# A gated-layer kernel: inner products in two more places, and the weight sums they need made one chunk earlier

## The chip, the core and the metric

The kernel runs on one core of one Trainium2 chip. The metric is device time in microseconds of one execution, lower is better. The engines of the core are written as in the profile: PE (matrix products), PEld (its weight loads), DVE (element-wise work on tensors), ACT (activations and copies), POOL (a second element-wise engine), SP (issues most DMAs). A tile has 128 partitions; "128x512" means 128 partitions by 512 elements.

## The reference

Four layers in a row on 2048 tokens of width 1024, each with a layer norm ahead of it and a residual behind it: linear attention, gated layer, linear attention, gated layer. Both attention layers share their weights, and both gated layers share theirs.

```python
def _B_ref(x, W_gate, W_up, W_down):          # the gated layer, F = 3584
    gate = einsum("bsd,df->bsf", x, W_gate)
    up = einsum("bsd,df->bsf", x, W_up)
    gate = gate * (gate > 0)
    return einsum("bsf,fd->bsd", gate * up, W_down)

x = x + _A_ref(_layernorm(x), A_wqkv, A_wo)   # layer 0 in the kernel
x = x + _B_ref(_layernorm(x), ...)            # layer 1
x = x + _A_ref(_layernorm(x), A_wqkv, A_wo)   # layer 2
x = x + _B_ref(_layernorm(x), ...)            # layer 3
```

## The kernel before

**Stages.** `run` calls `layer_A(0)`, `layer_B(1)`, `layer_A(2)`, `layer_B(3)`. A gated layer works on two chunks of 1024 tokens. This text writes (1,0) for the first chunk of layer 1, (1,1) for its second, and (3,0), (3,1) for those of layer 3. In each chunk there are 14 units `u` of 256 hidden columns (`glu`), and then the product with `W_down` (`down`), which adds its results onto the residual `x`.

**A unit.** Gate and up (`g` and `u` in names) are 2x2 block products in Winograd's form: seven block products instead of eight, numbered 1 to 7, each with one of seven combinations of weight blocks and of activation blocks (`s1` to `s4` are sums of activations). One block product is a group of four matmuls of 128x512 (`mm`, L1264). A unit is therefore 14 groups, in the order 5g 1g 5u 1u 2g 6g 2u 6u 7g 3g 7u 3u 4g 4u. The results pass through PSUM banks X, Y and Z: ACT copies X to Y (L1306), DVE makes Z from Y and product 5 (`zg`, `zu`, L1320), DVE adds product 5 to Y after product 7 (`m5g`, `m5u`, or `c22g`, `c22u` where product 5 comes from SBUF, L1340), and DVE's `put` (L1291) writes `h`. Because product 7 goes onto the same Y that Z is made from, group 7g must not start before `zg` is made, nor 7u before `zu`; and 4g and 4u must not start before `m5g` and `m5u` have read Y.

**Inner products.** In some units product 5 or 6 is not made by its own groups. For a pair of units (u, u+1) it is a 2x2 block product in itself, and is made by Winograd's form once more: seven inner products (`inner_gi`, L1117), each a group of four matmuls of 128x256, spread over the unit before the pair. They take the place of four groups of 128x512. The table `INNER` says where: product 5 in (3,0) for units 4 to 13 and in (3,1) for units 2 to 13; product 6 in (3,1) for units 3 to 12. Where product 6 comes from SBUF, DVE makes Y as X plus it (L1304) in place of ACT's copy.

Inner products need weight sums of a pair. `make_gi` makes them: eight DVE subtractions of 128x256 (L1072), DMAs of parts that exist already (`gi<-w`, L1075 and L1078), and one store of the subtractions' results (L1080). They are kept in DRAM as `gi5_u` and `gi6_u`, and `load_gi` (L1101) brings 896 KB of them back for each pair. Before the change the `gi5` are made in (1,1), with the still unused half of an `h` tile as the place of their results (named `h` in the profile), and the `gi6` in (3,0). `ready_gi` sets up a user of inner products: where the loaded sums lie, where results go (`V`), and four DVE sums of activations. For the places it uses tiles of `x` that have been sent away to DRAM (`send_away`, L274) and are brought back later (`bring_back`, L277).

**Weights.** In (1,0), `make_gu` makes a unit's four sums of weight blocks (L1172 to L1175, DVE) a unit ahead, and stores them as `tg`, `tu`. Later chunks load raw blocks (L1161) and sums (L1165); the sum that only product 5 or 6 uses is not loaded where that product is an inner one. Weights stand in a ring, five entries ahead.

**Order.** Code is written in the order of PE's work. `later.at(n, ...)` puts an action n ticks ahead, and a tick is one group of `mm`. `behind(last_put, ...)` asks that an action be scheduled after the last `put` made so far. A scheduler then fixes each engine's order when the program is built. DVE's order is thus a list that is known ahead of time, and so is SP's list of DMAs.

**Norms.** The layer norm ahead of layer 2 needs mean and variance of each 128-token tile `x[t]`: two `BATCH_NORM_STATS2` of 128x512 (L166) and one aggregate (L198). Before the change this was asked for from `down` of (1,1); the instructions for the first eight tiles stand among units 7 to 9 of (1,1), 564 to 591 us.

Of the kernel before, what the change touches and what calls it, by code (L numbers as in the profile page):

```python
# [14 lines left out]
P = 128  # L15
NW = 512
# [54 lines left out]
class _Later:  # L71
# [5 lines left out]
    def at(self, delay, fn):  # L77
        self.n += 1
        self.tasks.append((self.now + delay, self.n, fn))
# [13 lines left out]
class _Net:  # L93
# [93 lines left out]
    def ln_norm(self, layer, t):  # L187

        nc = self.nc
        if layer % 2:  # L190
            return self.ln_norm_sums(layer, t)
        src = self.xb[t] if layer == 0 else self.x[t]
        stats = self.small.tile([P, 2, nc.vector.BN_STATS_DIM], F32, tag="stats")
        for c in range(2):
            self.ln_stat(t, src, c, stats)
        if layer == 2:
            mv = self.small.tile([P, nc.vector.BN_AGGR_DIM], F32, tag="mv")
            nc.vector.bn_aggr(out=mv, in_=stats)  # L198
        else:
            mv, rstd = self.ln_rstd(stats)  # L200

        def scale(rstd=None if layer == 2 else rstd):
            if rstd is None:
                with self.tc.issue_after(self.last_exp.ins):
                    rstd = self.ln_root(mv)
                return lambda: scale(rstd)
            if layer % 2 == 0 and (layer, t // QT) != (2, 0):
                return self.ln_scale(src, mv, rstd, self.xn_home(layer, t))
            xn = self.temp([P, self.D], F16, name="xnb") if layer % 2 else self.xn_home(layer, t)
            shift = self.small.tile([P, 1], F32, tag="shift")  # L210
# [6 lines left out]
        return scale  # L217

    def ln_norm_sums(self, layer, t):

# [827 lines left out]
        for n in range(4):  # L1048
            self.later.at(at + 18 + 4 * n, lambda n=n: self.behind(self.last_put, lambda n: self.sums_dd(p, n), (n,)))

    INNER = {(3, 0): {5: range(4, 14)}, (3, 1): {5: range(2, 14), 6: range(3, 13)}}
    T_GU = {5: 0, 6: 2}

    def is_inner(self, l, c, u):
# [5 lines left out]
    def make_gi(self, l, c, m, u, at, out):  # L1060

        O = out.rearrange("p (n w k f) -> p n w k f", n=4, w=2, f=P)
        gi = self.gi[m, u]

        def block(w, a):
            return self.sums_gu(self.ring.get((l, c, w, u + a)))[:, self.T_GU[m]]

        def sums(n, w):
            b1, b2 = (block(w, a) for a in range(2))
            (b11, b21), (b12, b22) = ([b[:, 2 * j:2 * j + 2, :] for j in range(2)] for b in (b1, b2))  # L1070
            for o, a, b in ((0, b12, b11), (2, b22, b12), (1, b22, O[:, 0, n]), (3, b21, O[:, 1, n])):
                self.nc.vector.tensor_tensor(out=O[:, o, n], in0=a, in1=b, op=ALU.subtract)  # L1072

        for n, w in enumerate("gu"):
            self.later.at(at + n, lambda n=n, w=w: self.nc.sync.dma_start(  # L1075
                out=gi[:, 4:6, n, :, :], in_=block(w, 0).rearrange("p (j k) f -> p j k f", j=2)))
            self.later.at(at + 2 + 2 * n, lambda n=n, w=w: self.behind(self.last_put, lambda n: sums(n, w), (n,)))
            self.later.at(at + 4 + n, lambda n=n, w=w: self.nc.sync.dma_start(  # L1078
                out=gi[:, 6, n, :, :], in_=block(w, 1)[:, 2:4, :]))
        self.later.at(at + 6, lambda: self.nc.sync.dma_start(out=gi[:, 0:4, :, :, :], in_=O))  # L1080

# [496 lines left out]
    def plan_inner(self, l, c, u, hT):  # L1578

        at = self.later.at  # L1580
        ready = lambda m, *homes: self.behind(self.last_put, lambda m: self.ready_gi(l, c, m, *homes), (m,))
        if (l, c) == (1, 1):
            if u % 2 == 0 and u > 1:
                self.make_gi(l, c, 5, u, 2, hT[u // 2][:, 4:8, :].rearrange("p a n -> p (a n)"))
        if (l, c) == (3, 0):
            if u == 0:
                for n in range(4):
                    at(1 + 2 * n, lambda t=self.NS + n: self.send_away(t))
            if u == 2:
                self.inner_s = self.slot("gs", [P, 8 * NW], F16)  # L1590
                at(6, lambda: ready(5, 10, 8, self.inner_s[:, 0:4 * NW]))
            if u % 2 and 2 < u < self.U - 1:
                self.make_gi(l, c, 6, u, 2, self.inner_s[:, 4 * NW:8 * NW])
# [12 lines left out]
    def layer_B(self, l, final):  # L1606
        ring = self.ring
# [5 lines left out]
        for c in range(2):  # L1613
            hT = []
            first = l == 1 and c == 0
            wd = {}
            for u in range(self.U):
                if u % 2 == 0:
                    hT.append(self.slot(f"h{l}_{c}_{u // 2}", dtype=F16))
                ring.load_to(ring.index((l, c, "g", u)) + 5)  # L1620
                if first:
                    if u + 1 < self.U:
                        for n, w in enumerate("gu"):
                            self.later.at((4 if u else 9) + 4 * n, lambda u=u, w=w: behind(
                                self.last_put if u else self.last_z,
                                lambda: self.make_gu(ring.get((l, c, w, u + 1)), w, u + 1)))
                    if u == 3:
                        for d in (self.U - 4, self.U - 2):
                            wd[d] = self.load_d(d)
                        self.make_dd("22", 18)  # L1630
                    if u in (4, 5, 6):
                        for i, n in enumerate(range(3 * (u - 4), min(3 * (u - 3), 8))):
                            self.later.at(2 + 4 * i, lambda d=self.U - 4 + n // 4 * 2, n=n % 4: behind(
                                self.last_put, lambda: self.sums_d(wd[d], d, (n,))))
                    if u == 7:
                        self.make_dd("T1", 1)
                if not final and c == 1:
                    if u in (0, 3):
                        self.load_w("qk"[u // 3])
                    if u in (1, 2, 4, 5):  # L1640
                        for n in range(2):
                            self.later.at(4 + 5 * n, lambda w="qk"[u // 4], n=2 * (u % 3 - 1) + n: behind(
                                self.last_put, lambda: self.sums_w(w, n)))
                self.plan_inner(l, c, u, hT)
                if (l, c, u) in ((1, 1, 6), (3, 0, 5)):
                    self.make_dd("T4" if l == 1 else "21", 1)
                if c == 0 and u == 1:
                    for n, turn in enumerate(self.turns):
                        self.later.at(1 + n, turn)
                if c == 0 and u in (1, 2):  # L1650
                    self.later.at(6, lambda u=u: behind(self.last_put, self.pairs[u - 1]))
                self.glu(l, c, u, hT)
                if c == 0 and u == 2:
                    self.pairs[2]()
                if c == 0 and u == (self.U - 1 if first else 0):
                    after = self.last_put.ins
                if c == 1 and u == 6:
                    held = self.last_put.ins
            if c == 0:
                self.ln_chunk(l, 1, 20, 3, 3, after)  # L1660
            elif not final:
                self.ln_later(l + 1, 0, 24, 3, 4, held)
# [62 lines left out]
```

## Time and profile before

| | us |
|---|---|
| three runs | 1442.39, 1441.43, 1442.41 (median 1442.39) |
| the profiled execution, its own time | 1442.3 |
| its span, first to last instruction | 1440.5 |
| (1,1), 14 units, from 478.9 to 650.3 | 171.4 |
| (1,1), DVE busy in 479.08 to 650.58 | 100.39 |
| (1,1), DMA: bytes moved between 479 and 602 | 42.21 MB, 343 GB/s |

A line of the timeline reads: start, busy time, engine, line, operation, out<-in, count, and in brackets the idle time of the engine just before and what ended it. PE's busy times overlap, so the start of a group and the start of the next one give its cost. A line of the windows reads: the stretch, its length, then the busy time of each engine with its number of instructions, the granted clock, the DMA share (the mean over 16 engines; packets overlap, so it can pass 1) and GB/s. The granted TensorE clock is 1.000 over the whole span.

### The profile page before, as it was taken

What the parts mean: (1) busy time and instruction counts of PE and PEld (TensorE: products, weight loads), DVE (VectorE), ACT (ScalarE), POOL (GpSimd) and SP (SyncE); (2) the same over time, 40 slices, a digit from 0 to 9 for tenths busy, and PEclk for the clock granted to TensorE, in tenths of its full rate; (3) what the DMA queues carried; (4) which work ended last, traced back from release to release, by engine and by line L of the source; (5) the groups of instructions that cost most, each with busy time, mean ns of one, the idle gap of its engine ahead of it and who ended that gap; (6) DMA issues with size and microseconds to landing.
All of it is one profiled execution on the core that took longest, in us unless ns stands there. A gap on an engine that the chain in (4) does not pass through costs nothing.

```text
span 1440.5 us, 20916 instructions
## 1 busy us (share of the span) xinstructions
PE 1431.3 (99%) x7592; PEld 728.0 (51%) x7622; DVE 1014.4 (70%) x1951; ACT 619.1 (43%) x1129; POOL 309.9 (22%) x221
## 2 busy tenths in 40 slices
PE   9999999999999999999999999999999999999998
PEld 4444444444455444445654444444544565555457
DVE  7978698677594466649778885865655864666695
ACT  7872564333334234332058725733443433444200
POOL 1453860010000011010031477410111011111102
PEclk9999999999999999999999999999999999999999
DMA  9950787998459999845973119996977798755565
GB/s 291 235 162 8 174 208 206 289 320 275 166 195 298 341 353 332 283 154 191 296 275 99 62 23 239 284 293 220 297 241 242 224 303 273 232 183 183 174 236 181
DMA packets 345591, 325.52 MB, mean 226 GB/s; under 512 B 108720, under 2 KB 306608, under 8 KB 344464
## 3 DMA queue, kind: packets, MB, share of 16 engines
q1 hardware_dynamic: 337440, 302.89, 69.8%
q10 hardware_dynamic: 6560, 17.24, 3.2%
q0 software_dynamic: 1488, 4.07, 0.9%
q8 instruction: 59, 0.97, 0.3%
q14 instruction: 44, 0.36, 0.1%
HBM read 235.67 MB, written 63.83 MB: 208 GB/s over the span
## 4 chain that ended last, share of the span: by engine, by line
PE 93%; DVE 4%; ACT 1%; issue 1%; DMA 0%; DVEq 0%; SPq 0%; ACTq 0%
PE ps L497 11%; PE yu L1264 9%; PE yg L1264 9%; PE dy L1404 8%; PE xg L1264 6%; PE xu L1264 6%; PE dx L1404 6%; PE ps L780 4%; PE i L1117 3%; PE zg L1264 3%; PE zu L1264 3%; PE my L579 3%; PE dyT L1456 2%; PE vu L1264 2%; PE mv L579 2%; PE mx L579 2%
## 5 line engine op out<-in xcount | busy, mean ns | idle before, releaser
L1264 PEld LDWEIGHTS <-w 128*128 128x128 f16 (+1 forms) x2880 | 281.4, 98 | 320.0 <-issue 5.2
L497 PE MATMUL ps<-w,xnT 128*128 128x512 bf16 x768 | 169.8, 379 | 0.2 <-DVE pq L443 0.2
L1344 POOL TENSOR_TENSOR h<-m5u,m5g 128x512 f16<-128x512 f32 x34 | 44.7, 1316 | 487.8 <-DVE m5u L1340 376.9
L497 PEld LDWEIGHTS <-xnT 128*128 128x128 bf16 x768 | 74.4, 98 | 89.8 <-issue 1.8
L1264 PE MATMUL xu<-xnT,w 128*128 128x512 f16 x448 | 115.0, 379 | 0.5 <-ACT yu L1306 0.5
L1264 PE MATMUL xg<-xnT,w 128*128 128x512 f16 x448 | 114.9, 379 | 0.0
L1404 PEld LDWEIGHTS <-h 128*128 128x128 f16 x672 | 65.8, 98 | 78.2
L1264 PE MATMUL yu<-s,w 128*128 128x512 f16 x408 | 104.7, 379 | 0.6 <-DVE zu L1320 0.5
L1264 PE MATMUL yg<-s,w 128*128 128x512 f16 x408 | 104.9, 379 | 0.1
L1456 PEld LDWEIGHTS <-h 128*128 128x128 f16 x966 | 94.5, 98 | 12.4
L440 ACT ACTIVATE e<-e,eps 128x512 f32<-128x512 f32 x128 | 90.9, 720 | 3.2
L727 POOL TENSOR_TENSOR kvc<-pq,kvc 128x1024 f32<-128x1024 bf16 x32 | 78.5, 2454 | 53.1 <-DVE den L732 32.8
L1404 PE MATMUL dx<-w,h 128*128 128x512 bf16 x381 | 84.7, 379 | 0.6
L780 PE MATMUL ps<-T,pqT 128*128 128x512 bf16 x374 | 83.0, 379 | 0.5
L1320 DVE TENSOR_TENSOR zg<-yg,m5g 128x512 f32<-128x512 f32 x34 | 23.7, 698 | 84.4 <-PE yg L1264 80.5
L1344 POOL TENSOR_TENSOR h<-c22u,c22g 128x512 f16<-128x512 f32 x22 | 28.0, 1271 | 229.0 <-DVE c22u L1340 197.2
L1291 DVE TENSOR_TENSOR h<-yu,r 128x512 f16<-128x512 f32 x56 | 38.6, 689 | 54.5 <-PE yu L1264 54.5
L1288 ACT ACTIVATE r<-yg 128x512 f32<-128x512 f32 x56 | 33.4, 597 | 97.9 <-PE yg L1264 97.9
L518 POOL TENSOR_TENSOR kvc<-kvc,slab 128x512 f32<-128x512 f32 x46 | 57.2, 1250 | 75.9 <-DVE slab L443 72.7
L439 ACT ACTIVATE e<-ps 128x512 f32<-128x512 f32 x92 | 54.3, 590 | 29.3 <-PE ps L497 28.8
L1288 ACT ACTIVATE r<-zg 128x512 f32<-128x512 f32 x56 | 32.9, 588 | 73.0 <-PE zg L1264 73.0
L739 POOL TENSOR_TENSOR pq<-pq,den 128x1024 bf16<-128x1024 bf16 x32 | 61.2, 1911 | 6.8 <-DVE den L734 6.8
(267 smaller groups left out, 2557.0 us busy)
## 6 DMA issues: line engine op xcount, KB each, us to landing
w<-in_B_W_gate_dram SPq DMA_DIRECT2D x56, 512.0 KB, 6.4
w<-in_B_W_up_dram SPq DMA_DIRECT2D x56, 512.0 KB, 6.2
w<-ddT SPq DMA_DIRECT2D x21, 896.0 KB, 6.4
w<-td SPq DMA_DIRECT2D x18, 896.0 KB, 4.9
w<-dd SPq DMA_DIRECT2D x15, 896.0 KB, 5.7
w<-in_B_W_down_dram SPq DMA_DIRECT2D x14, 896.0 KB, 5.0
away<-x SPq DMA_DIRECT2D x20, 512.0 KB, 8.2
w<-tg SPq DMA_DIRECT2D x20, 512.0 KB, 8.4
```

Source lines behind the costliest of these rows:

```text
L440: self.last_exp = nc.scalar.activation(out=e, in_=e, func=ACT.Exp, scale=-1.0, bias=self.eps6[:, 0:1])
L497: nc.tensor.matmul(by_row(ps), lhsT=self.xnT[l, l_q][:, kt, j * P:(j + 1) * P], rhs=w[:, kt, :].rearrange("p (b i d) -> p i b d", i=R, d=H ...
L518: nc.gpsimd.tensor_tensor(out=ksum[:, cols], in0=ksum[:, cols], in1=pk, op=ALU.add)
L579: nc.tensor.matmul(banks[j], lhsT=A(i)[:, j * P:(j + 1) * P], rhs=B(i), start=start and i == 0, stop=i == NS - 1, skip_group_check=True)
L727: nc.gpsimd.tensor_tensor(out=prod, in0=pq_of[sc, j], in1=zrow, op=ALU.mult)
L739: nc.gpsimd.tensor_tensor(out=heads(pq), in0=heads(pq), in1=den[:, :].unsqueeze(2).to_broadcast([P, D // HD, HD]), op=ALU.mult)
L780: nc.tensor.matmul(ps, lhsT=pqT[sc][:, g, j * P:(j + 1) * P], rhs=T[g // 4][:, g % 4, n2 * NW:(n2 + 1) * NW], start=(g == 0), stop=(g == G ...
L1264: nc.tensor.matmul(ps, lhsT=W[w][m][:, k, :], rhs=A[m][:, k, :], start=start and k == 0, stop=k == 3, skip_group_check=True)
L1288: self.last_relu = nc.scalar.activation(out=out, in_=ps, func=ACT.Relu)
L1344: nc.gpsimd.tensor_tensor(out=h[:, 3, :], in0=V["u"], in1=V["g"], op=ALU.mult)
L1404: nc.tensor.matmul(banks[j], lhsT=A(k)[:, j * P:(j + 1) * P], rhs=w[:, i, :], start=start and k == 0, stop=k == self.U - 1, skip_group_che ...
L1456: nc.tensor.matmul(bank[:, j * H:(j + 1) * H], lhsT=A[i // 2][:, i % 2, j * P:(j + 1) * P], rhs=B[m][:, i, :], start=start and i == 0 and ...
```

## The change

Product 5 becomes an inner product in (1,1) for units 4 to 13, and product 6 in (3,0) for units 5 to 12. For that, the `gi5` are made in (1,0) and the `gi6` in (1,1), each one chunk earlier. In (1,1) the places are tiles of `x` (`x[0]` to `x[4]`, and `x[7]` for the subtractions of `gi6`), which hold the first chunk's residual and have a copy in DRAM; they are brought back at the end of (1,1). Their norm statistics are made before they are overwritten (`ln_early`) and kept in `acc`. In (3,0) tiles 12 to 15 are sent away and brought back in addition.

```diff
+        if layer == 2 and t < self.NS:
+            mv = self.acc[:, 2 * t:2 * t + 2]
         else:
-            mv, rstd = self.ln_rstd(stats)
+            stats = ...
...
+    def ln_early(self, t):
+        stats = self.small.tile([P, 2, self.nc.vector.BN_STATS_DIM], F32, tag="stats")
+        for c in range(2):
+            self.ln_stat(t, self.x[t], c, stats)
+        self.nc.vector.bn_aggr(out=self.acc[:, 2 * t:2 * t + 2], in_=stats)
...
-    INNER = {(3, 0): {5: range(4, 14)}, (3, 1): {5: range(2, 14), 6: range(3, 13)}}
+    INNER = {(1, 1): {5: range(4, 14)}, (3, 0): {5: range(4, 14), 6: range(5, 13)},
+             (3, 1): {5: range(2, 14), 6: range(3, 13)}}
...
-            self.later.at(at + 2 + 2 * n, lambda n=n, w=w: self.behind(self.last_put, lambda n: sums(n, w), (n,)))
-            self.later.at(at + 4 + n, lambda n=n, w=w: self.nc.sync.dma_start(
+            self.later.at(at + 2 + 3 * n, lambda n=n, w=w: self.behind(self.last_put, lambda n: sums(n, w), (n,)))
+            self.later.at(at + 3 + 3 * n, lambda n=n, w=w: self.nc.sync.dma_start(
...
+        if (l, c) == (1, 0):
+            if u % 2 == 0 and u > 1:
+                self.make_gi(l, c, 5, u, 4, rest)
         if (l, c) == (1, 1):
-            if u % 2 == 0 and u > 1:
-                self.make_gi(l, c, 5, u, 2, hT[u // 2][:, 4:8, :].rearrange("p a n -> p (a n)"))
+            if u % 2 and 2 < u < self.U - 1:
+                self.make_gi(l, c, 6, u, 2, self.x[7].bitcast(F16))
+            if u == 0:
+                for t in range(self.NS):
+                    at(4 + 2 * t, lambda t=t: self.behind(self.last_put, self.ln_early, (t,)))
+            if u == 2:
+                at(5, lambda: ready(5, 2, 0, 4))
+            if u == self.U - 2:
+                for t in range(2, self.NS):
+                    at(t, lambda t=t: self.bring_back(t))
         if (l, c) == (3, 0):
...
             if u == 2:
-                self.inner_s = self.slot("gs", [P, 8 * NW], F16)
-                at(6, lambda: ready(5, 10, 8, self.inner_s[:, 0:4 * NW]))
-            if u % 2 and 2 < u < self.U - 1:
-                self.make_gi(l, c, 6, u, 2, self.inner_s[:, 4 * NW:8 * NW])
+                s = self.slot("gs", [P, 8 * NW], F16)
+                self.inner_s = [s[:, n * NW:(n + 4) * NW] for n in (0, 4)]
+                at(6, lambda: ready(5, 10, 8, self.inner_s[0]))
+            if u == 3:
+                for n, t in enumerate((14, 15, 12, 13)):
+                    at(1 + 2 * n, lambda t=t: self.send_away(t))
+                at(9, lambda: ready(6, 14, 12, self.inner_s[1]))
             if u == self.U - 2:
-                for t in range(2, 4):
-                    at(t, lambda t=t: self.bring_back(self.NS + t))
+                for n, t in enumerate((10, 11, 14, 15, 12, 13)):
+                    at(3 + 2 * n, lambda t=t: self.bring_back(t))
...
-                at(7 if u + 2 == us[0] else 1, lambda m=m: self.load_gi(m, u + 2))
+                at(10 if u + 2 == us[0] else 1, lambda m=m: self.load_gi(m, u + 2))
...
-            for n in range(2 if (l, c) == (3, 0) else 0):
-                self.later.at(2 + n, lambda t=n + self.NS: self.bring_back(t))
+            for n in range(2 if (l, c) in ((1, 1), (3, 0)) else 0):
+                self.later.at(2 + n, lambda t=n + (c == 0) * self.NS: self.bring_back(t))
```

In the built programs the change moves instructions as follows. In (1,0), in each even unit from 2 to 12, eight subtractions come into DVE's list: in units 2, 4, 8, 10 and 12 four stand ahead of `zg`, in unit 6 three ahead of `zg` and one just behind it; of the other four, three stand between `zu` and `m5g` and one between `m5g` and `m5u`. The store of their results (L1080) comes into SP's list after them, in unit 6 between the two parts of the load `ddT<-td`. In (1,1), four of the sixteen statistics instructions stand in `down` of (1,0) and twelve in units 0 and 1: in unit 0 DVE's list reads `zg`, `zu`, `m5g`, `h<-xu`, three statistics, an aggregate, a statistic, `m5u`, an aggregate, two statistics, `h<-zu`, an aggregate, two statistics, `h<-yu`, an aggregate, three statistics, an aggregate, a statistic, a sum of `wq`, an aggregate, and then `zg` of unit 1.

More of the change, by code (lines that the diff above doesn't have):

```diff
@@ L192, in ln_norm @@
         src = self.xb[t] if layer == 0 else self.x[t]
[L193 to L198, printed above, removed]
-        else:
-            mv, rstd = self.ln_rstd(stats)
+        if layer == 2 and t < self.NS:
+            mv = self.acc[:, 2 * t:2 * t + 2]
+        else:
+            stats = self.small.tile([P, 2, nc.vector.BN_STATS_DIM], F32, tag="stats")
+            for c in range(2):
+                self.ln_stat(t, src, c, stats)
+            if layer == 2:
+                mv = self.small.tile([P, nc.vector.BN_AGGR_DIM], F32, tag="mv")
+                nc.vector.bn_aggr(out=mv, in_=stats)
+            else:
+                mv, rstd = self.ln_rstd(stats)
         def scale(rstd=None if layer == 2 else rstd):
@@ L217, in ln_norm @@
         return scale
+    def ln_early(self, t):
+        stats = self.small.tile([P, 2, self.nc.vector.BN_STATS_DIM], F32, tag="stats")
+        for c in range(2):
+            self.ln_stat(t, self.x[t], c, stats)
+        self.nc.vector.bn_aggr(out=self.acc[:, 2 * t:2 * t + 2], in_=stats)
     def ln_norm_sums(self, layer, t):
@@ L1580, in plan_inner @@
         at = self.later.at
+        rest = hT[u // 2][:, 4:8, :].rearrange("p a n -> p (a n)")
         ready = lambda m, *homes: self.behind(self.last_put, lambda m: self.ready_gi(l, c, m, *homes), (m,))
+        if (l, c) == (1, 0):
+            if u % 2 == 0 and u > 1:
+                self.make_gi(l, c, 5, u, 4, rest)
         if (l, c) == (1, 1):
-            if u % 2 == 0 and u > 1:
-                self.make_gi(l, c, 5, u, 2, hT[u // 2][:, 4:8, :].rearrange("p a n -> p (a n)"))
+            if u % 2 and 2 < u < self.U - 1:
[8 more added lines that the diff above has]
+                    at(t, lambda t=t: self.bring_back(t))
         if (l, c) == (3, 0):
```

## The prediction

> **What bounds the kernel now.** I read the totals and the chain of waits first.
>
> ```profile
> span 1440.5 us, 20916 instructions
> PE 1431.3 (99%) x7592; PEld 728.0 (51%) x7622; DVE 1014.4 (70%) x1951; ACT 619.1 (43%) x1129; POOL 309.9 (22%) x221
> PE 93%; DVE 4%; ACT 1%; issue 1%; DMA 0%; DVEq 0%; SPq 0%; ACTq 0%
> ```
>
> PE's stream sets the time; no other engine's sum comes near. So there are two questions: how much PE work goes, and where PE will newly stand still. For the first I went to PE's timeline, (3,0), where product 5 is an inner product already.
>
> ```profile
> 1041.63 1.03 PE L1264 MATMUL yu<-xnT,w 128*128 128x512 f16 x4
> 1042.49 0.60 PE L1117 MATMUL i<-s,x 128*128 128x256 f16 x4
> 1042.93 0.81 PE L1264 MATMUL xg<-xnT,w 128*128 128x512 f16 x3
> ```
>
> Start to start, a plain group costs 0.86 us (0.8635 over longer stretches) and an inner one 0.44 (0.436). For the second I took DVE's timeline in (1,0) and (1,1), and the windows of whole units, which show how full DVE and the DMA engines are.
>
> ```profile
> 275.64:287.95 12.31, 12.31 (x59) 5.59 (x58) 8.97 (x16) 4.64 (x8) 1.27 (x1) 1.00 0.93 309
> 300.05:312.20 12.15, 12.15 (x57) 5.43 (x56) 11.42 (x19) 5.11 (x9) 3.18 (x2) 1.00 1.03 301
> 479.08:491.33 12.25, 12.25 (x58) 5.58 (x57) 4.81 (x8) 4.67 (x8) 1.27 (x1) 1.00 1.05 380
> ```
>
> After the length come PE, PEld, DVE, ACT, POOL. Units 4 and 6 of (1,0) have DVE busy 8.97 of 12.31 and 11.42 of 12.15 us, and this is where the new subtractions go. Unit 0 of (1,1) has 4.81 of 12.25, but its order decides, not its sum.
>
> **A: PE work that goes.** Nine pairs of units lose four plain groups and gain seven inner ones: five in (1,1), four in (3,0). By groups that is 4 x 0.8635 - 7 x 0.436 = 0.40 a pair, 3.6 in all. By whole pairs it is less: a plain pair is 28 x 0.8635 = 24.18; with product 5 inner, 1019.11 to 1042.93 is 23.82; with 5 and 6, in (3,1), 1244.34 to 1267.81 is 23.47, with small waits of 0.10 in it. So 5 x 0.36 + 4 x 0.35 = 3.2. I take -3.2, bounds -3.6 to -3.2.
>
> The Trainium skill has a rule that speaks against this step: "TensorE: Matmul & The Clock Gate", section "Back-to-back issue gap", gives a sustained stream about 81 ns a matmul at 128 columns and 131 ns at 512, from which I estimate 98 ns at 256. By that, 16 x 131 ns = 2.10 us would be replaced with 28 x 98 ns = 2.74 us, and nine pairs would lose 5.8 us. The rows here give 216 ns (0.8635 / 4) and 109 ns (0.436 / 4); they decide.
>
> **B: stalls of (1,1) that go.** (1,1) lasts 171.4 us; 14 units of 14 groups make 169.25 us, and about 1.75 us of the excess shows as gaps ahead of PE groups: 0.17, 0.17, 0.17, 0.15 and 0.20 in units 1 to 7, and the largest here:
>
> ```profile
> 566.04 1.87 DVE L166 BATCH_NORM_STATS2 stats<-x 128x6 f32<-128x512 f32 x3
> 582.30 1.02 PE L1264 MATMUL xu<-xnT,w 128*128 128x512 f16 x4 [0.51 <-ACT yu L1306]
> ```
>
> Those in units 7 to 9 (0.20 + 0.67 + 0.21 = 1.1) stand where statistics run, which leave; some of the others go with product 5's own groups. I take -1.3, bounds -0.5 and -1.75. The first line also prices a statistic: three in 1.87, 0.60 each in a row.
>
> **C: subtractions in (1,0).** Price, from (1,1), where the same ones run before:
>
> ```profile
> 552.96 0.28 DVE L1072 TENSOR_TENSOR h<-w,w 128x256 f16<-128x256 f16 x1
> 553.15 0.28 DVE L1072 TENSOR_TENSOR h<-w 128x256 f16<-128x256 f16 x1
> ```
>
> 0.20 from start to start, so eight make 1.6 us per even unit. What they delay shows in unit 6:
>
> ```profile
> 306.10 0.41 DVE L1175 TENSOR_TENSOR w<-w 128x512 f16<-128x512 bf16 x1
> 306.43 0.69 DVE L1320 TENSOR_TENSOR zg<-yg,m5g 128x512 f32<-128x512 f32 x1
> 308.23 0.69 DVE L1320 TENSOR_TENSOR zu<-yu,m5u 128x512 f32<-128x512 f32 x1
> 309.16 0.68 DVE L1340 TENSOR_TENSOR m5g<-yg,m5g 128x512 f32<-128x512 f32 x1
> ...
> 307.17 1.02 PE L1264 MATMUL yg<-s,w 128*128 128x512 f16 x4
> ```
>
> DVE runs without a gap up to `zg`, which ends at 307.12, and 7g follows at once. In unit 4, `m5u` moves back by the 0.8 that DVE lacks and ends 0.23 after 4u is due: +0.3. In unit 6, `zg` comes behind that and three subtractions (0.6): +0.6; the one behind it delays `zu` by 0.2, and the rest `m5g` by 0.1: +0.9 in all. In unit 8 three stand ahead of `m5g` (334.29 before, already at its limit): +0.6. In units 2, 10 and 12 DVE idles often enough. Sum +1.8, bounds +0.8 (unit 6 and others regain time in PE's own delay) and +3.
>
> **D: the store from `h`.** The results lie in `h`, so the store must land before `put` writes there in the next unit; this is a wait of `h<-xu`, and behind it on DVE stand a weight sum and `zu`, for which 7u waits. Such a wait exists before: DVE waited for `gi` stores twice.
>
> ```profile
>   DVE h L1291: 1.4, 2
> ...
> gi<-h SPq DMA_DIRECT2D x6, 512.0 KB, 4.0
> ```
>
> Unit 6's store is the latest. On SP's list it stands behind `gi<-w` copies (which wait for weight sums), a gate load, and the first part of `ddT<-td` (which waits for `td` stores that land at 312.65), so it is issued at about 314.1. Its user is here:
>
> ```profile
> 318.52 0.69 DVE L1291 TENSOR_TENSOR h<-xu,r 128x512 f16<-128x512 f32 x1 [0.17 <-PE xu L1264]
> ...
> ddT<-td SPq DMA_DIRECT2D x1, 896.0 KB, 7.0
> ddT<-td SPq DMA_DIRECT2D x1, 768.0 KB, 9.5
> tg<-w ACTq DMA_DIRECT2D x2, 512.0 KB, 6.4
> ```
>
> With the delays of C and the slack of `zu`, landing up to about 320.1 is free. The row `gi<-h` (4.0, in (1,1)) makes that 0; `tg<-w`, a store of the same size in the same stretch, lands at 320.5: +0.4; `ddT<-td` gives +1.2 or, by 9.5, +3.5. I take +0.4, bounds 0 and +3.5. The second `ddT<-td`, behind it on SP, is used only at 325.8.
>
> **E: statistics at the start of (1,1).** Unit 0 of before:
>
> ```profile
> 487.49 0.68 DVE L1291 TENSOR_TENSOR h<-xu,r 128x512 f16<-128x512 f32 x1
> 488.61 0.69 DVE L1340 TENSOR_TENSOR m5u<-yu,m5u 128x512 f32<-128x512 f32 x1 [0.44 <-PE yu L1264]
> ...
> 490.14 1.03 PE L1264 MATMUL yu<-xnT,w 128*128 128x512 f16 x4
> ```
>
> From 488.09, where `h<-xu` lets go, come three statistics, an aggregate and a statistic: 4 x 0.60 + 0.11 = 2.5. `m5u` then runs 490.6 to 491.3, and 4u, due 490.14, starts 1.2 later; behind `m5u` on DVE, `h<-zu` and `h<-yu` follow in time. In unit 1 the list up to `zg` ends at 499.57, against 499.07 for 7g: +0.5. Sum +1.7, bounds +0.6 (a statistic runs while `m5u` could not start yet) and +2.5.
>
> **Costed at nothing.** Loads `x<-gi` in (1,1) and for product 6 in (3,0): in (1,1) each is issued at the end of an odd unit, 13 groups ahead of use, 13 x 0.8635 = 11.2 us; the row `x<-gi` has 5.9, and loads between 479 and 602 land in 2.5 to 10.9. Past 11.2, each us costs one. In (3,0) the first lands at about 994 and is used at 998.8. Tiles sent away and brought back move while the DMA share is 0.34 to 0.57. The sums `ready_gi` and `gi6` in (1,1), less `gi5` there, fall on a DVE with 4.8 of 12 us taken; (3,0) loses its subtractions. Statistics in `down` of (1,0) fall in DVE's gaps of 0.3 to 0.8 us. Weight loads land 8 to 16 us ahead of use.
>
> **Sum.** -3.2 - 1.3 + 1.8 + 0.4 + 1.7 = -0.6: span 1439.9. The profiled execution took 1442.3, 1.8 more than its span, and the median of the runs is 1442.39; so 1441.7. All bounds together: -3.6 - 1.75 + 0.8 + 0 + 0.6 = -4.0, and -3.2 - 0.5 + 3 + 3.5 + 2.5 = +5.3.
>
> **Rivals.**
> 1. DVE's new work is absorbed: C 0.8, D 0, E 0.6, with -1.75 in B: -3.6 or -4.0, 1438.4 to 1438.8. For it: DVE is busy 70%, and PE, once late, gives DVE time back, so delays do not add up. Against: `zg` of unit 6 and `m5u` of unit 0 stand in lists without a gap.
> 2. Slower: stores from `h` hold up `put`. Place: `h<-xu` of units 7 and 9. If landing takes 9.5 us, as the slower `ddT<-td`, unit 7 pays 3.5 instead of 0.4 and unit 9 (store issued about 337.5, user 342.84 plus 1.5 of delay and some slack) about 2: -0.6 + 5.1 = +4.5, time 1446.9. It decides from landings of about 8.5 us, where the sum passes 1445. For: DMA share is 1.03 there, SP is late. Against: all 512 KB rows of that stretch show 5.3 to 6.5.
> 3. Slower: `x<-gi` in (1,1) lands late, 13 us in three of the pairs: 3 x 1.8 = 5.4, time 1447.1; against it, the 10.9 seen at most.
> 4. Inner products save nothing where weights are read at share 1.05, so that A is 0: time 1444.9. Against: weights land early.
>
> **How the numbers follow.** Forecast 1441.7 with its own range 1439.5 to 1444: chance 0.44. Rival 1: 0.29. Rival 2: 0.16. Rival 3: 0.04, rival 4: 0.03, others, slower, 0.04. Measurement tells about 0.2%, 2.9 us, from no change: faster lies below 1439.5, slower above 1445.3. Faster is rival 1 with a little of the forecast, 0.30; slower is 2, 3 and the others, 0.24; the rest 0.46. The range of 8 in 10 takes in most of rival 1 and rival 2's near half: 1438.2 to 1446.4.
>
> **What would show it.** A: pairs in (1,1) at 23.8 us and in (3,0) at 23.5. B: no gap ahead of `xu` at unit 8 or 9 of (1,1). C: 7g of unit 6 in (1,0) waiting for `zg` by 0.5 or more. D: `h<-xu` of unit 7 waiting for a DMA. E: 4u of (1,1)'s unit 0 waiting for `m5u` by about 1.2 us. I am wrong if (1,0) grows by more than 4 us or not at all, or if pairs in (1,1) keep 24.2 or more.

## The result, and the profile after

| | before | after |
|---|---|---|
| median of six runs, us | 1442.24 (1441.43 to 1442.63) | 1447.55 (1445.43 to 1450.04) |
| ratio after to before | | 1.0037, 95% interval 1.0024 to 1.0050 |
| span of the profiled execution | 1440.5 | 1445.8 |
| (1,0), 14 units | 182.95 | 190.24 |
| (1,1), 14 units | 170.99 | 169.82 |
| (3,0), 14 units | 130.50 | 129.29 |

The change made the kernel 5.3 us slower. The runs also scatter more: 4.6 us between the ends after, 1.2 before. The stage lengths run from the first PE group of the units to the first of `down`; the other stages differ by 0.3 us or less. So the two stages that should gain have gained 1.2 us each, and (1,0), where the sums are now made, has lost 7.3.

The totals and the chain of waits after the change (line numbers are higher by 10 from the table `INNER` on):

```profile
span 1445.8 us, 21272 instructions
PE 1432.8 (99%) x7730; PEld 739.2 (51%) x7730; DVE 1037.7 (72%) x1993; ACT 622.5 (43%) x1138; POOL 310.0 (21%) x221
PE 90%; DVE 4%; DMA 2%; ACT 1%; issue 1%; SPq 1%; DVEq 0%; ACTq 0%
```

PE's busy sum went up, although PE has less to do, and the chain now has a DMA share of 2%. A busy sum that grows with less work means that the same instructions took longer. The windows of the three stages (length, then PE, PEld, DVE, ACT, POOL, the granted clock, DMA share, GB/s) say where; (1,0) and (1,1) of before come first:

```profile
214.01:396.96 182.95, 182.10 (x839) 82.03 (x840) 132.02 (x234) 70.73 (x122) 18.49 (x14) 1.00 0.81 251
478.92:649.91 170.99, 170.38 (x786) 76.64 (x785) 99.98 (x186) 66.78 (x120) 17.78 (x14) 1.00 0.88 290
```

```profile
214.12:404.36 190.24, 185.42 (x842) 82.78 (x841) 140.88 (x282) 71.26 (x122) 18.50 (x14) 0.98 0.86 270
486.31:656.13 169.82, 168.02 (x845) 82.42 (x844) 102.72 (x184) 67.83 (x121) 17.80 (x14) 1.00 0.97 315
987.32:1116.61 129.29, 129.29 (x722) 70.48 (x721) 79.86 (x122) 54.44 (x97) 13.98 (x11) 1.00 0.82 265
```

In (1,0), PE idles for 4.8 us (0.85 before) and the granted clock is 0.98 (1.00 before). DVE's timeline in unit 7 shows the first:

```profile
318.00 0.70 DVE L1330 TENSOR_TENSOR zg<-yg,m5g 128x512 f32<-128x512 f32 x1 [2.33 <-PE yg L1274]
323.65 0.69 DVE L1301 TENSOR_TENSOR h<-xu,r 128x512 f16<-128x512 f32 x1 [4.95 <-DMA gi<-h]
324.26 0.68 DVE L1182 TENSOR_TENSOR w<-w 128x1024 f16<-128x1024 bf16 x1
324.86 0.69 DVE L1330 TENSOR_TENSOR zu<-yu,m5u 128x512 f32<-128x512 f32 x1
```

`h<-xu` waits 4.95 us for the store of `gi5_6`; behind it, in DVE's order, come a weight sum and `zu`. PE's timeline shows who waits for `zu`:

```profile
320.54 1.03 PE L1274 MATMUL zg<-s,w 128*128 128x512 f16 x4
325.61 1.87 PE L1274 MATMUL yu<-s,w 128*128 128x512 f16 x4 [4.04 <-DVE zu L1330]
327.26 1.91 PE L1274 MATMUL zu<-s,w 128*128 128x512 f16 x4
328.97 1.91 PE L1274 MATMUL yg<-xnT,w 128*128 128x512 f16 x4
330.68 1.42 PE L1274 MATMUL yu<-xnT,w 128*128 128x512 f16 x4
```

7u starts 4.20 us after it could. Then a second loss follows, which no wait shows: the next groups start 1.65 to 1.71 us apart instead of 0.86; the four from 325.61 to 331.93, where the fifth starts, take 6.32 us instead of 4 x 0.8635 = 3.45, 2.87 us more. Windows of 3.41 us over that place:

```profile
321.22:324.63 3.41, 0.34 (x2) 0.07 (x1) 0.97 (x2) 0.60 (x1) 0.00 (x0) 1.00 1.03 406
324.63:328.04 3.41, 2.44 (x6) 0.86 (x6) 2.71 (x6) 0.63 (x1) 0.00 (x0) 0.50 1.14 344
328.04:331.46 3.42, 3.42 (x9) 1.22 (x8) 0.85 (x2) 0.48 (x1) 1.26 (x1) 0.50 1.04 352
```

The clock is halved for two stretches of 3.41 us, beginning a good 3 us after PE fell idle and going on while it works again. So one late store costs 4.20 + 2.87 = 7.1 us. When it was issued, and how long it took (DMA issues between 313.6 and 316.6; the last number is us to landing):

```profile
ddT<-td SPq DMA_DIRECT2D x1, 896.0 KB, 7.5
...
gi<-h SPq DMA_DIRECT2D x1, 512.0 KB, 9.3
tg<-w ACTq DMA_DIRECT2D x1, 512.0 KB, 7.9
```

The store was issued at 314.24 and landed at 323.5.

### The profile page after: what moved, and what is told of

The parts are those of the page before. It is cut to its first block, busy times and chain, and to the rows that moved or that the text cites. A ratio compares the mean times of both kernels' runs of the same rounds, so it can differ in the third digit from the quotient of the medians.

```text
span 1445.8 us, 21272 instructions
## 1 busy us (share of the span) xinstructions
PE 1432.8 (99%) x7730; PEld 739.2 (51%) x7730; DVE 1037.7 (72%) x1993; ACT 622.5 (43%) x1138; POOL 310.0 (21%) x221
## 4 chain that ended last, share of the span: by engine, by line
PE 90%; DVE 4%; DMA 2%; ACT 1%; issue 1%; SPq 1%; DVEq 0%; ACTq 0%
PE ps L506 11%; PE yu L1274 8%; PE yg L1274 8%; PE dy L1414 7%; PE xg L1274 6%; PE xu L1274 6%; PE dx L1414 6%; PE i L1127 5%; PE ps L789 4%; PE zu L1274 3%; PE zg L1274 3%; PE my L588 3%; PE dyT L1466 2%; PE mv L588 2%; PE mx L588 2%; PE dy L1466 2%
## 5 line engine op out<-in xcount | busy, mean ns | idle before, releaser
L1274 PEld LDWEIGHTS <-w 128*128 128x128 f16 (+1 forms) x2736 | 268.2, 98 | 295.2 <-issue 12.4
L1354 POOL TENSOR_TENSOR h<-m5u,m5g 128x512 f16<-128x512 f32 x24 | 32.0, 1335 | 387.2 <-DVE m5u L1350 220.2
L1354 POOL TENSOR_TENSOR h<-c22u,c22g 128x512 f16<-128x512 f32 x32 | 40.7, 1271 | 334.6 <-DVE c22u L1350 291.8
L1274 PE MATMUL yu<-s,w 128*128 128x512 f16 x376 | 97.3, 381 | 4.9 <-DVE zu L1330 4.9
L1274 PE MATMUL yg<-s,w 128*128 128x512 f16 x376 | 96.8, 379 | 0.0
L1127 PEld LDWEIGHTS <-x 128*128 128x128 f16 x560 | 54.7, 98 | 38.8 <-DMA x<-gi 2.0
L1120 ACT ACTIVATE x<-i 128x512 f32<-128x512 f32 x75 | 44.7, 595 | 46.2 <-PE i L1127 46.2
```

The source lines that it names most:

```text
L1127: nc.tensor.matmul(b[:, w, :], lhsT=B[p][:, w, k, :], rhs=A[p][:, k, :], start=start and w == 0 and k == 0, stop=k == 1, skip_group_check= ...
L1274: nc.tensor.matmul(ps, lhsT=W[w][m][:, k, :], rhs=A[m][:, k, :], start=start and k == 0, stop=k == 3, skip_group_check=True)
L1354: nc.gpsimd.tensor_tensor(out=h[:, 3, :], in0=V["u"], in1=V["g"], op=ALU.mult)
```

## The experiments

The theory: the loss in (1,0) is this one store, through the wait and the low clock behind it. The rivals: DVE is too full there, the low clock comes from something else, or the loss would only move. Times are medians; each has the runs of before on the same chip (1441.8 to 1442.4) beside it.

**The store from ACT's queue.**

```diff
-        self.later.at(at + 6, lambda: self.nc.sync.dma_start(out=gi[:, 0:4, :, :, :], in_=O))
+        q = self.nc.scalar if (l, c) == (1, 0) else self.nc.sync
+        self.later.at(at + 6, lambda: q.dma_start(out=gi[:, 0:4, :, :, :], in_=O))
```

> The six stores of the subtractions' results in (1,0) are issued from ACT's queue instead of SP's; nothing else. Theory (store of unit 6 is late, 7u of unit 7 waits 4.0 us for it through h<-xu and zu, and the granted clock falls for about 6 us afterwards, 2.9 us more): on ACT the store is issued once its last subtraction is done, about 311.7 instead of 314.24, ahead of the ddT<-td loads, and lands by about 318.5 to 319.5; wait of 7u under 0.5 us, no stretch with a granted clock under 0.9, (1,0) takes 183.3 to 184 us instead of 190.2, time about 1440.5. Rival 1 (DVE too full in units 6 and 7, the store only the last of several things that are late): a wait of 1 us or more stays before 7u or moves to m5g, time 1443 to 1446. Rival 2 (the clock falls because of what PE does, not because it stood still): the wait goes but some 2.9 us at a low clock stay, time about 1443.5.

Measured: 1444.89 us (1442.67 to 1447.16), ratio 1.0018 (1.0009 to 1.0028). In the profiled execution, which at 1442.67 is the fastest of its ten, the store is issued at 313.55 and lands after 6.2 us; 7u starts 0.3 us late instead of 4.2, and (1,0) takes 185.51 us. But in unit 8, PE waits 1.9 us for `yu`, which ACT makes:

```profile
331.73 0.33 ACTq L1187 DMA_DIRECT2D tg<-w  x1
332.11 0.58 ACT L1317 ACTIVATE yu<-xu 128x512 f32<-128x512 f32 x1 [3.46 <-DMA ddT<-ddT]
```

ACT has to issue a store ahead of the copy, and by the profile stands there until another DMA has landed. In this execution the clock stays at 1.0 in (1,0), though PE does the same work, which speaks against rival 2. Three of the ten runs show a mean clock of 0.998, so low clock may be left in some. By the medians 3.0 us of the loss of 5.3 remain. That is rival 1's time but not its reason: what waits now is ACT, not a DVE that is too full.

**The store ahead of the ddT loads, still on SP.** `load_dd` is put behind the store with `behind`.

> The store stays on SP, but the ddT<-td loads are put behind it on SP's list; nothing else. Theory that the landing is late because of the 896 KB load issued just ahead of it on the same queue: store issued about 313.7, lands about 319.5 (near the gate load's 5.5 to 6 us), wait of 7u under 0.7, no low clock, time 1440.5 to 1441.5. Rival (all DMA engines are full there, share 1.0, and order makes no difference): landing stays 8.5 to 9.5 us after issue, wait about 3.5 us, clock falls again, time 1446 to 1447.

Measured: 1444.19 us (1441.25 to 1449.60), ratio 1.0020 (1.0009 to 1.0031). In the profiled execution the store is now issued at 315.73, lands after 8.2 us, and 7u waits 4.3 us, with one stretch of 3.41 us at half clock. The DMA issues from 314.8 to 317:

```profile
w<-in_B_W_gate_dram SPq DMA_DIRECT2D x1, 512.0 KB, 8.1
gi<-h SPq DMA_DIRECT2D x1, 512.0 KB, 8.2
```

A load issued just ahead of it took as long, so the 896 KB ahead on the queue are not what makes a landing slow. The rival's wait and low clock are there, at a time between theory and rival: the loss against the runs of before is 2.3 us instead of 5.3, so order does something; what, one profile does not tell.

**Pair 6 left out.** Units 6 and 7 of (1,1) keep plain groups, and `gi5_6` is made in (1,1): `{5: (4, 5, 8, 9, 10, 11, 12, 13)}`.

> Units 6 and 7 of (1,1) keep product 5 as plain groups, and the sums gi5_6 are made in (1,1) as before the change; the other four pairs stay. (1,0) then has no subtractions in unit 6 and no store that must land in unit 7. Theory: (1,0) takes about 183.3 us, no low clock; (1,1) is 0.36 longer by the lost pair and keeps a wait for x<-gi of up to 1.5 us somewhere; time about 1441. Rival (the other stores or the fuller DVE of (1,0) cost too): (1,0) stays above 185 us, time 1443 or more.

Measured: 1441.07 us (1438.60 to 1443.11), ratio 0.9990 (0.9980 to 0.9999). In the profiled execution (1438.60, the lowest of its runs) (1,0) takes 182.91 us: five of six `gi5` are still made there and nothing is lost. Taking out unit 6's alone gives back 7.3 us of (1,0). The other runs are up to 4.5 us longer, so in some of them something still waits.

**Another place for unit 6's results.** They go into the `h` tile of units 8 and 9, made two units sooner.

> The results of unit 6's subtractions go into the unused h tile of units 8 and 9 (made two units sooner for it) instead of the second half of the tile that unit 7 writes; so h<-xu of unit 7 no longer waits for the store, and its reuse comes two units later. Theory: no wait in unit 7 whatever the landing, no low clock, (1,0) about 183.5 us, time about 1440.5. Rival 1 (the store would be late for someone anyway, or the tile that the ddT<-td load now takes becomes free late): a wait in units 7 to 10 of (1,0) of over 1 us, time over 1442. Rival 2 (clock falls by itself): 2.9 us at a low clock stay, time 1443.5.

Measured: 1447.34 us (1446.22 to 1450.60), ratio 1.0039 (1.0025 to 1.0053). The store lands after 6.3 us and nothing waits for it, but (1,0) takes 189.49 us, nearly as long as with the wait: others are there, among them, on DVE's timeline:

```profile
330.58 1.09 DVE L1051 TENSOR_TENSOR ddT<-ddT 128x1792 f16<-128x1792 f16 x1 [1.85 <-DMA ddT<-ddT]
...
338.95 0.69 DVE L1182 TENSOR_TENSOR w<-w 128x1024 f16<-128x1024 bf16 x1 [3.55 <-DMA w<-in_B_W_up_dram]
```

7u of unit 8 waits 3.1 us. The theory, that the place alone would do, fell; rival 1's wait and time came, with other transfers late instead. That they are late because the tile was taken from something else is likely and not shown. The longest wait, 3.1 us, brought no half clock.

**Stalls of several lengths, in the kernel before.** `zu` is repeated in odd units of (3,0), `{1: 3, 3: 4, 5: 5, 7: 6, 9: 8, 11: 10, 13: 14}` times more.

> The kernel before the change, with zu of units 1, 3, 5, 7, 9, 11 and 13 of (3,0) made several times over (3, 4, 5, 6, 8, 10 and 14 repeats of the same instruction, 0.60 us each, into the same place), so that 7u stands still for different lengths; the result is the same. Theory (a PE that stands still for about 4 us or more gets half the clock for one or more stretches of 3.4 us; 3.1 us, seen in an experiment, cost nothing more): waits of up to about 3 us are followed by groups at 0.86 us, waits of 4 us and more by groups at 1.7 us for 3.4 us or twice that. Rival (the low clock in the changed kernel comes from its greater weight loading, not from standing still): no stretch at half clock here before the last 5 us of the span.

Measured: one run of 1460.04 us. PE's idle times came out as 1.4, 2.2 and 3.7 us in units 7, 9 and 11; in the other units PE was given other groups to do in between. Half clock came twice, for 3.41 us each, and the two beginnings, 1072.12 and 1102.84, are 9.00 times 3.41 apart. Cut on that grid:

```profile
1068.71:1072.12 3.41, 1.27 (x6) 0.49 (x5) 3.27 (x5) 0.58 (x1) 0.00 (x0) 1.00 0.85 261
1072.12:1075.53 3.41, 3.31 (x8) 1.13 (x8) 1.35 (x3) 0.60 (x1) 0.50 (x1) 0.50 0.08 25
1096.02:1099.43 3.41, 1.78 (x9) 0.69 (x7) 3.24 (x6) 0.58 (x1) 0.00 (x0) 1.00 0.91 272
1099.43:1102.84 3.41, 1.33 (x7) 0.62 (x7) 2.16 (x4) 0.00 (x0) 0.00 (x0) 1.00 1.06 362
1102.84:1106.25 3.41, 3.41 (x12) 1.52 (x11) 2.41 (x4) 0.60 (x1) 1.27 (x1) 0.50 0.15 58
```

PE is the first column after the length, the clock the third from the end. A stretch in which PE is busy for 1.27 or 1.33 us is followed by half clock (the second line and the last), one with 1.78 is not. The theory's lengths were wrong: 2.2 us of idling is enough when it falls into one stretch, and 3.1 us (the experiment before) is not when it falls across two. The rival, weight loading, fell: this is the kernel before. That it was the same in the changed kernel is seen above: 0.34 us busy, then half clock.

**Only the part in (3,0).** `INNER` without (1,1), `gi5` made in (1,1) as before; product 6 in (3,0) and the early statistics stay.

> The changed kernel without inner products in (1,1): gi5 are made in (1,1) as before, (1,0) has no subtractions; product 6 in (3,0), gi6 made in (1,1) and the early statistics stay. Theory by the terms of the prediction: (3,0) 1.2 to 1.4 us shorter, (1,1) shorter by the stalls of 1.3 to 1.75 that the statistics made, (1,0) at 183.0 as before: time about 1439.3. Rival (the fuller DVE and DMA of (1,1) cost what the stalls gave): (1,1) at 171 us, time about 1441.

Measured: 1439.91 us (1439.77 to 1441.25), ratio 0.9987 (0.9978 to 0.9996).

```profile
214.07:397.05 182.98, 182.20 (x841) 82.00 (x840) 132.10 (x234) 70.73 (x122) 18.52 (x14) 1.00 0.80 251
479.01:648.52 169.51, 169.51 (x786) 76.62 (x784) 107.86 (x218) 66.02 (x116) 18.27 (x14) 1.00 1.02 337
```

(1,1) is 1.48 us shorter with no inner product in it, and PE is busy in it throughout: the stalls of before are gone with the late statistics. The runs lie close together.

**The price alone.** All `gi5` made in (1,0), none used in (1,1).

> All six gi5 are made in (1,0) as in the changed kernel, but (1,1) has no inner products; (1,1) then reads the sums from nowhere, and all else is as in the changed kernel. It shows the price of the move by itself. Theory: (1,0) shows the same wait of 7u in unit 7 for the store, 2 to 4.5 us, with a stretch at half clock in most runs; against the run with gi5 made in (1,1) (1439.9) some 4 to 8 us more, so 1444 to 1448, spread of 3 us and more. Rival (the wait needs the inner products of (1,1) in some way): time under 1442.

Measured: 1447.24 us (1445.73 to 1450.31), ratio 1.0036 (1.0024 to 1.0049).

```profile
214.17:402.51 188.34, 184.13 (x840) 82.48 (x840) 140.97 (x282) 71.26 (x122) 18.51 (x14) 0.99 0.87 273
...
325.17:328.58 3.41, 3.41 (x10) 1.21 (x9) 1.81 (x5) 0.63 (x1) 1.10 (x1) 0.50 1.15 346
```

The same wait in the same place (3.3 us of idling), and half clock behind it, for one stretch. Against the experiment before it, which differs in where `gi5` are made, that is 1447.24 - 1439.91 = 7.3 us (7.1 when each is taken against its own runs of before). Not all of it is the store: in the profiled executions (1,0) is 5.4 us longer, and (1,1) 1.9 (171.37 against 169.51), where PE waits 1.5 us for a load `w<-tu`.

**The waiting instruction behind `zu`.** In unit 7 of (1,0) `h<-xu` is put after `zu` with `behind`.

> The changed kernel with one change of order on DVE: in unit 7 of (1,0) h<-xu, which waits for the store, stands behind zu instead of ahead of it (and the weight sum that stood between them goes ahead of zg). The store is as late as before. Theory (the landing costs through what is queued behind the waiting instruction): 7u starts in time; m5g is now behind the wait, so 4g, due 1.7 us after 7u, waits 1.5 to 2 us instead of 4.0, too short for a stretch at half clock; (1,0) about 185.3, time 1442 to 1443. Rival (PE waits for the store itself or for the DMA engines): wait of about 4 us stays, time 1447.

Measured: 1443.21 us (1440.22 to 1446.16), ratio 1.0006 (0.9997 to 1.0015).

```profile
318.96 0.69 DVE L1182 TENSOR_TENSOR w<-w 128x1024 f16<-128x1024 bf16 x1 [3.49 <-issue]
...
321.51 0.69 DVE L1330 TENSOR_TENSOR zu<-yu,m5u 128x512 f32<-128x512 f32 x1
324.85 0.69 DVE L1301 TENSOR_TENSOR h<-xu,r 128x512 f16<-128x512 f32 x1 [2.65 <-DMA gi<-h]
325.46 0.68 DVE L1352 TENSOR_TENSOR m5g<-yg,m5g 128x512 f32<-128x512 f32 x1
```

The store is later than ever, and PE idles only 0.9 us for `m5g` behind it; 7u does not wait. It loses another 2.2 us at 7g, because the weight sum, now ahead of `zg`, stood still until 318.96; that is this experiment's own doing, and (1,0) takes 187.32 us instead of the 185.3 expected. The expected 1.5 to 2 us at 4g was too much, the median lies 0.2 us above the forecast range, and no half clock came in this execution. What the late landing costs is decided by what stands behind the waiting instruction.

**Two places for the loaded sums, four pairs.** As with pair 6 left out; the loads `x<-gi` of (1,1) go to `x[2..3]` and `x[5..6]` in turn.

> As the experiment with pair (6,7) plain, and the sums that inner products of (1,1) read have two places (x[2..3] and x[5..6] in turn), so that the loads of pairs 8, 10 and 12 can be issued a unit or more sooner and no longer wait for the pair before. Theory (what varies from run to run there is the landing of x<-gi, 0 to 1.5 us of waiting in (1,1)): no wait for x<-gi in (1,1), median near the lowest run of the earlier experiment, 1438.6, spread under 2 us. Rival (the spread has another source): median stays about 1441.

Measured: 1440.32 us (1438.27 to 1443.09), ratio 0.9986 (0.9977 to 0.9995). No wait for `x<-gi` is in its profile, but that is an execution of 1438.47, near the fastest. The spread is 4.8 us (4.5 without the second place), which speaks against the loads as its source, and the median lies between theory and rival. Where the scatter comes from is not shown.

**Only the pairs made late in (1,0)**, 10 and 12.

> Inner products in (1,1) for pairs 10 and 12 alone; only their sums are made in (1,0), in units 10 and 12, the others in (1,1) as before the change. Theory (the making of gi5 costs only where (1,0) has DMA engines full, up to about 345 us): (1,0) 183.0 us, (1,1) 0.7 shorter than with no inner products there (168.8), time about 1439.2 with a spread under 1 us. Rival (any store and copies in (1,0) make its time vary): median 1440 or more, spread of 2 us and more.

Measured: 1442.76 us (1440.95 to 1446.00), ratio 1.0003 (0.9994 to 1.0012). (1,0) is 182.98, but (1,1) takes 171.4: the first pair's load is issued only four groups ahead of its use. From PE's list of waits:

```profile
PE i L1127 <- DMA x<-gi: 0.8, 1, 0.8
```

This wait, at 598 us, and two behind it for ACT (0.7 and 0.4) with what stands around them are 2.3 us of lost time, so the experiment told nothing of its question. It was made again with the loads a unit sooner and two places:

> As the experiment with pairs 10 and 12 alone, which brought its first pair in only four groups ahead of use (the wait of 0.8 us for x<-gi and what followed it, 2.3 us in all, was that experiment's own fault); here the loads go into two places in turn and are issued a unit sooner. Theory (gi5 may be made in (1,0) where DMA engines are not full): no wait for x<-gi, (1,1) 168.8 to 169.1, (1,0) 183.0, time 1439.2 and spread under 1.5 us. Rival (making them costs by itself wherever it is): median 1440 or more with a spread of 3 us.

Measured: 1439.90 us (1438.98 to 1441.41), ratio 0.9985 (0.9976 to 0.9994).

```profile
214.00:396.96 182.96, 182.10 (x840) 82.07 (x840) 134.89 (x250) 70.96 (x122) 18.49 (x14) 1.00 0.83 261
478.92:647.86 168.94, 168.89 (x810) 79.00 (x808) 106.73 (x210) 66.52 (x118) 17.90 (x14) 1.00 1.01 332
```

Two `gi5` made after 345 us cost nothing in (1,0), and (1,1) is 0.57 us shorter than without inner products. The time is level with that of the part in (3,0) alone; the spread, 2.4 us, lies between the theory's 1.5 and the rival's 3.

**With pair 8 too**, made in unit 8.

> The same with pair 8 too: its sums are made in (1,0) in unit 8, between 324 and 345 us, where DMA engines are full. Theory: gains 0.36 more in (1,1), but the time varies as in the experiments with four pairs, so a median of 1439.5 to 1441 and a spread over 2 us. Rival (unit 6's store is the only one that costs): 1438.8 with a spread under 1.5 us.

Measured: 1440.41 us (1439.41 to 1443.33), ratio 0.9989 (0.9980 to 0.9998). More pairs, no better time, and a spread of 3.9 us, as the theory had it. The gain of 0.36 did not show: in the profiled execution (1,1) takes 169.45 us, 0.5 more than with two pairs, and PE waits there 0.7 us for DVE's work on inner products. What waits in the longer runs was not seen: the profiled executions of these kernels are not among their longest.

## Why the prediction was wrong

It forecast 1441.7 us, range 1438.2 to 1446.4; measured 1447.55. One of its own signs of being wrong came: (1,0) grew by more than 4 us, by 7.3. By its steps, in the profiled executions (forecast, then measured):

- **A, -3.2: right.** Pairs in (3,0) take 23.49 us (1020.98 to 1044.47, between two 3g groups) and pairs without a wait in (1,1) 23.80 (568.37 to 592.17). That makes 4 x 0.30 (the stage lost 1.21) + 5 x 0.38 = 3.1. The rows of 216 and 109 ns held. The 131 ns that the Trainium skill, "TensorE: Matmul & The Clock Gate", section "Back-to-back issue gap", states for 512 columns, and the estimate of 98 ns for 256, did not.
- **B, -1.3: right.** The run with (3,0) alone shows 1.48 us less in (1,1) with no other gain there, E's waits included. The 171.4 us that the text ahead of the prediction gives for (1,1) are 0.4 too many: the first group of `down` starts at 649.91, so the stage took 170.99, and the gaps of 1.75 us were all of its excess.
- **C, +1.8: too much.** 3g of unit 7 starts at 320.54 instead of 319.98, and 0.11 of that was there before unit 0: +0.45. The delays of DVE were right in place; the step failed in holding PE's order fixed. In the program after the change PE's order is another too: single matmuls of the next unit's 5g stand ahead of 7g, 7u, 4g and 4u where these would wait. The trace before shows the same at the very place that was read as 7g following at once. PE's timeline in unit 6, before and then after, where 7g would have been due at 307.11:

```profile
306.92 0.38 PE L1264 MATMUL vg<-s,w 128*128 128x512 f16 x1
...
307.11 0.38 PE L1274 MATMUL vg<-s,w 128*128 128x512 f16 x1
307.53 1.02 PE L1274 MATMUL yg<-s,w 128*128 128x512 f16 x4
```

- **E, +1.7: the same mistake.** `m5u` came as late as forecast (497.94 is 490.55 in the times of before, since (1,1) now starts 7.39 later), and 4u did not wait. DVE's timeline in unit 0 of (1,1):

```profile
495.49 1.87 DVE L166 BATCH_NORM_STATS2 stats<-x 128x6 f32<-128x512 f32 x3
...
497.94 0.67 DVE L1350 TENSOR_TENSOR m5u<-yu,m5u 128x512 f32<-128x512 f32 x1
```

  And PE's:

```profile
497.54 1.03 PE L1274 MATMUL vg<-s,w 128*128 128x512 f16 x4
498.40 0.38 PE L1274 MATMUL xg<-xnT,w 128*128 128x512 f16 x1
498.67 1.02 PE L1274 MATMUL yu<-xnT,w 128*128 128x512 f16 x4
```

  Between 4g and 4u stand the next unit's 5g and the first matmul of its 1g, five matmuls that need nothing new. Later waits for `zg` in unit 1 and `zu` in unit 2 cost 0.24 in all.
- **D, +0.4: this step failed.** The mechanism, its place and the issue at about 314.1 (measured 314.24) were right; the size was not. I took the 6.4 us of `tg<-w` for the landing, and it was 9.3, close to the slower `ddT<-td` (9.5) that stood as upper bound and in rival 2. By that bound the term would have been 3.5, and it was 4.20: a landing was to be free up to 320.1 with 1.2 us of C's delays counted in, and since only 0.45 came of these it was free up to about 319.3. And a term was missing altogether: 2.87 us at half clock after the stall. Sum 7.1 instead of 0.4. (The step's middle value is off by a little too: by its own row of 7.0 it is +1.0, not +1.2.)
- **Costed at nothing, and not nothing:** `x<-gi` of pair 10. I gave it 11.2 us of cover by counting 13 plain groups; the load was issued at 588.65 (on SP a load `w<-tg`, whose issue took 1.9 us, and a `ddT` store stand ahead of it) and due at about 597.4, so 8.7, and it landed after 10.3:

```profile
598.99 0.61 PE L1127 MATMUL i<-x 128*128 128x256 f16 x4 [1.46 <-DMA x<-gi]
```

  With a late `zu` in unit 4, (1,1) paid 1.6 + 0.5 us, which took back what its five pairs had gained.

Added up, with E inside B's 1.48: -3.1 - 1.5 + 0.45 + 7.1 + 2.1 = +5.05, of the 5.3 us by which the spans differ.

Rival 2 named the place and nearly the price of the first half; its second place, unit 9, did not wait at all: that store landed after 4.8 us, not 9.5, and with pair 6 left out, where unit 7 does not stall, after 4.7, and `h<-xu` did not wait for it there either. So its 1446.9 came near the measured time by luck, with the half clock in the place of unit 9's 2 us. Rival 1's absorption did happen, for C and E, by PE's order. Rival 3's wait came in one pair of five, by a load that was issued late and took 10.3 us, not 13. Rival 4 fell with A.

That the wait and its half clock made the loss of (1,0) is shown by three runs together: with the sums of unit 6 taken out, (1,0) is back at 182.91; with all six sums made there and not used, it is 5.4 us longer with the same wait; and with `h<-xu` behind `zu` the store is as late, but 7u does not wait and no half clock follows. That the stretch has room for the sums of unit 6 without any loss is not shown: every variant that keeps them there has other waits.

Open: why landing takes 9.3 us there. The same store took 8.7 and 8.4 in two other experiments, 8.2 ahead of the `ddT<-td` loads, but 6.3 with the other place, also ahead of them, and 6.2 from ACT's queue 0.7 us sooner. DMA share is 1.03 to 1.14 around it. Open too is what waits in the longer runs of the variants that make four pairs' sums in (1,0).

The fastest versions leave the (1,1) part out or keep two late pairs of it: 1439.9 us, 0.9987 and 0.9985 of before. Four pairs with two places (0.9986) cannot be told from them by the ratio, but scatter more.

## What to carry to other kernels

Where a transfer must land before an instruction of an in-order queue, price it with the slowest landing of that stretch of the trace, not the median, and add what stands behind the instruction. If the order of the other engines is made anew when the program is built, read their lists too before costing a delay: here delays by DVE's work were filled with other groups, and the two longest waits that remained were for transfers. That the builder takes these for shorter than they are is a guess. A wait of PE of over 2 us is to be costed at its length plus what half clock may follow: here nothing after one of 3.1 us, one stretch (some 1.7 us) after those of 2.2, 3.3, 3.7 and 4.3, and two (2.87 us) after the one of 4.0.

## What the hardware showed beyond that

The clock is judged in stretches of 3.41 us that do not follow the work. The half clock at the end of each trace, when PE has run out of work, begins a whole number of them after the earlier ones (in the changed kernel 1444.20 - 324.63 = 328.0 x 3.413), so the grid can be laid over a run that has no other. A stretch with PE busy for 0.34, 1.27 or 1.33 us was followed by half clock; on that grid the emptiest stretch without it is the first of these, with the store on ACT's queue; the second, little fuller, is with the other place for the results:

```profile
329.25:332.67 3.42, 1.57 (x8) 0.59 (x6) 1.66 (x5) 0.56 (x2) 0.00 (x0) 1.00 1.06 320
332.67:336.08 3.41, 3.34 (x16) 1.56 (x16) 2.21 (x5) 0.52 (x2) 0.00 (x0) 1.00 1.05 321
```

```profile
338.61:342.02 3.41, 1.71 (x8) 0.77 (x8) 3.07 (x6) 0.00 (x0) 0.00 (x0) 1.00 0.65 191
342.02:345.43 3.41, 3.08 (x15) 1.36 (x14) 3.41 (x8) 1.71 (x3) 1.27 (x1) 1.00 0.85 298
```

1.57 and 1.71 us of work kept the next stretch at full clock, so the limit lay between 1.33 and 1.57 here; no full-clock stretch of the kept traces falls on the wrong side of it. The way out of half clock took more work: full clock came back after stretches with 3.31 us of work or more, and not after the one with 2.44 in the changed kernel, where 7u started 1 us into it. That fits why its one stall cost two stretches. The Trainium skill, "TensorE: Matmul & The Clock Gate", section "What's actually happening", states a free-running window of 3413 ns; this case agrees. Its section "HAM oscillation — how this bites in real kernels" says that idle gaps above about 3.4 us are to be avoided; here 2.2 us were enough where they lay in one window, and 3.1 us across two were not. So the same late store can cost more in one run than in another, by where the stall falls on the grid. The mean granted clocks of the changed kernel's runs fit that, from 0.996 (1450.04 us) to 0.999 (1445.43 us), but only one of them has a trace here.
